# Attention and two feed-forward layers on one core: the order of the five queues comes from an event calculation instead of from hand-set delays

## The chip, the cores and the metric

The kernel runs on one core of a Trainium2 chip. A core has five engines with a queue of instructions each: TensorE (PE, matrix products), ScalarE (ACT), VectorE (DVE), GpSimd (POOL) and SyncE (SP), which here issues all transfers. Each queue is worked off strictly in the order in which it was written, and an instruction whose input or buffer isn't ready holds up all that stands behind it. The metric is the device time of one execution in microseconds (us), the median of several runs. Lower is better.

## The reference: what is computed

```
scores = q @ k.T / sqrt(64)            # q, k, v: 4 batches x 12 heads x 448 x 64
scores = cap * tanh(scores / cap)
attn   = exp(scores - max);  attn = attn / (sum(attn) + 1e-9)
x  = (attn @ v), heads side by side    # 1792 tokens x 768
h  = relu(x @ w_in);         y = (h * h) @ w_out              # 768 -> 2048 -> 768
gate = sigmoid(y @ w_gate);  val = y @ w_val                  # 768 -> 1536
out  = (gate * val) @ moe2_w_out                              # 1536 -> 768
```

The weights come as 64-bit numbers and are turned into 32-bit numbers on the chip.

## The kernel before, in words

The 48 heads are worked in 24 pairs. For a pair there are four steps of scores (on PE, 112 to 128 keys at a time, then tanh and exp on ACT) and four steps of PV (probabilities times values, on PE). The values carry a column of ones, so PV also gives the sums by which a pair's result must be divided: the result is stored to DRAM (`xd`), the row of sums is loaded again (`sg`), DVE takes the reciprocals (`rr`), they are stored (`rd`), and result and reciprocals are loaded side by side, the reciprocals spread over 64 partitions, and multiplied (`normalize`).

The first 12 pairs (the lead) run alone. The tokens of the layers are worked in two passes. Pass 0 takes the first 768 tokens, in blocks of 256 and 512, and the other 12 pairs' 48 attention steps are strewn between its units; pass 1 takes the last 1024 tokens in two blocks of 512. A unit is one product on PE of 128 output features by a block: 6 (`prod_a`) or 4 (`unit_b`) tiles of 128x128 weights, three matmuls for each tile, since every operand is held as a rounded high part and the rest (`wh` and `wl`, the two halves of `xa` and `gx`). In pass 0 there are 82 weight tiles (keys). For each one `wdma` loads the 64-bit words, `wconv` makes 32-bit numbers of them (ACT takes the absolute value, L310, DVE does four operations, L311 to L316), `wkeep` stores the result for pass 1, and `wround` splits it (ACT rounds `wh`, L331, POOL subtracts `wl`, L332). Two buffers `raw` hold a weight from `wconv` until both `wkeep` and POOL are done with it, four buffers hold `wh` and `wl`. From pair 13 on the probabilities `pt` (`th` in a pair's last step) are split on DVE as well before PV may use them (`split_scores`, L186 and L187). PV has one accumulator of two banks, which is copied out after a pair's last step (L210 or L212), so the next pair's first PV waits for that copy.

All five queues are written by hand-set rules: `go(us, fn)` moves a clock on by an assumed PE time, `at(delay, fn)` puts a piece of work into a list that is run when the clock has passed its delay, and `weights(u, n)`, called before each unit, writes as many steps of the weights' chain as counters and two fixed delays allow. Nobody asks there whether a buffer is free or an engine busy. The attention steps are put in when the units so far have used up `ATT` = 0.84 of pass 0's assumed time, step by step (`due`).

Of the kernel before, what the change touches and what calls it, by code (L numbers as in the profile page):

```python
# [14 lines left out]
ALU = mybir.AluOpType  # L15

# [12 lines left out]
PT = 11  # L29
WB = 4  # L30
LEAD = 4
ATT = 0.84
# [7 lines left out]
HIGH = float(np.uint32(0x47EFFFFF).view(np.float32))  # L40


@with_exitstack
def attn_mlp_kernel(ctx: ExitStack, tc: tile.TileContext, qk, v, cap, w1, w2, wg, wv, wo, out):
# [10 lines left out]
    def open_pool(name, side):  # L55
        guard = tc.tile_pool(name=name, bufs=1, side=side)
        open_pools[name] = guard, guard.__enter__()
# [26 lines left out]

    st = {}
    more = tc.tile_pool(name="more", bufs=1, space=bass.MemoryType.PSUM, side="right")
    pools = {"more": more.__enter__()}
# [4 lines left out]
    def unit_bank():  # L92
        return pools["units"].tile([P, 512], F32, tag="pn", name="pn", bufs=4)
# [6 lines left out]

    def new_v1(i, dt):
        vt = T("att", "v1", [P, KC, 4, D], dt, NV)
        w = f32(vt) if dt != F32 else vt
        nc.gpsimd.memset(w[:, :, 1:3, :], 1.0)
        return vt

    def new_v2():
        vt = T("att", "v2", [P, KC, 3, D], F32R, NV)
        nc.gpsimd.memset(f32(vt[:, :, 1, :]), 0.0)
        return vt  # L110

    v32, v1, v2 = [], [], []
# [5 lines left out]
    rd = [[dr.tile([2, S], F32, name=f"rd_{b}_{p}") for p in range(NP)] for b in range(B)]  # L118
    RP, RN = 16, 2 * S // 16


    def early(b):
        return b < B // 2

    def pair_tile(n=2):
        return T("att", "pt", [P, 2, S], bufs=PT) if n == 2 else T("att", "th", [P, 1, S], bufs=3)

    def split_tile(n=2):
        return T("att", "pt", [P, 2, S], F32R, bufs=PT) if n == 2 else T("att", "th", [P, 1, S], F32R, bufs=3)


    def load_pair(b, p):
        qr = T("mlp0", "acc", [P, QK], bufs=CC) if early(b) else T("att", "qk", [P, QK], bufs=2)
        nc.sync.dma_start(out=qr, in_=qk[b, p])
        vr = None
        if not early(b):
            vr = T("att", "vr", [P, KC, 2, D])
            nc.sync.dma_start(out=vr, in_=v[b, p])
        st["raw", b, p] = qr, vr

    def load_v(b, p):
        i = (b * NP + p) % NV
        for j in range(2):
            nc.sync.dma_start(out=v32[i][:, :, 3 * j, :], in_=v[b, p][:, :, j, :])

    def split_pair(b, p):
        qr, vr = st.pop(("raw", b, p))
        hi = T("att", "qkh", [P, QK], F32R, 2)
        lo = T("att", "qkl", [P, QK], F32R, 2)
        if early(b):  # L150
            nc.vector.tensor_copy(hi, qr)
        else:
            nc.scalar.activation(out=hi, in_=qr, func=AF.Copy)
        nc.vector.tensor_tensor(out=lo, in0=qr, in1=f32(hi), op=ALU.subtract)
        st["qk", b, p] = hi, lo
        st["vr", b, p] = vr

    def split_v(b, p):
        i = (b * NP + p) % NV
        vr = st.pop(("vr", b, p))  # L160
        if vr is not None:
            va, vb = v1[i][:, :, 0::3, :], v2[i][:, :, 0::2, :]
            nc.scalar.activation(out=va, in_=vr, func=AF.Copy)
            nc.vector.tensor_tensor(out=vb, in0=vr, in1=f32(va), op=ALU.subtract)


    def scores(b, p, step):
        hi, lo = st["qk", b, p]
        n = 2 if step < 3 else 1
        rows = [slice(0, D), slice(D, P)] if step < 3 else [slice(0, P)]  # L170
        turn = (p + b * NP + step) % 3
        sc = bank2("so" if turn == 0 else "si", pools["more"]) if early(b) and turn < 2 else bank2("se")
        c0 = S + step * P
        for i, (w, a) in enumerate(((lo, hi), (hi, lo), (hi, hi))):
            for u, r in enumerate(rows):
                nc.tensor.matmul(out=sc[:, u, :S], lhsT=w[r, c0:c0 + P], rhs=a[r, :S], start=i == 0, stop=i == 2)
        t = pair_tile(n)
        nc.scalar.activation(out=t, in_=sc[:, :n, :S], func=AF.Tanh, scale=qs)
        nc.scalar.activation(out=t, in_=t, func=AF.Exp, scale=capa)
        st["p", b, p, step] = t, None  # L180

    def split_scores(b, p, step):
        t, _ = st["p", b, p, step]
        n = 2 if step < 3 else 1
        ph, pl = split_tile(n), split_tile(n)
        nc.vector.tensor_copy(ph, t)  # L186
        nc.vector.tensor_tensor(out=pl, in0=t, in1=f32(ph), op=ALU.subtract)  # L187
        st["p", b, p, step] = ph, pl

    def pv(b, p, step):  # L190
        i = (b * NP + p) % NV
        if step == 0:
            st["o", b, p] = bank2("pv")
        o = st["o", b, p]
        ph, pl = st.pop(("p", b, p, step))
        c = (step + 1) % KC
        terms = [(v32, ph)] if early(b) else [(v2, ph), (v1, pl), (v1, ph)]
        for n, (vt, pt) in enumerate(terms):
            for j in range(2):

                r, u = (slice(0, P), j) if step < 3 else (slice(j * D, (j + 1) * D), 0)
                x = j if vt is v2 else 2 * j
                w = vt[i][r, c, x:x + 2, :].rearrange("p x d -> p (x d)")
                nc.tensor.matmul(  # L204
                    out=o[:, j, :S], lhsT=w, rhs=pt[r, u], start=step == 0 and n == 0, stop=step == 3 and n == len(terms) - 1)
        if step < 3:
            return
        xe = st["xe", b, p] = pair_tile()
        if early(b):
            nc.vector.tensor_copy(xe, o[:, :, :S])  # L210
        else:
            nc.scalar.activation(out=xe, in_=o[:, :, :S], func=AF.Copy)  # L212

    def store_pair(b, p):
        xe = st.pop(("xe", b, p))
        for j in range(2):
            r0, e0 = (XR, D - 1) if j else (1, 0)
            nc.sync.dma_start(out=xd[b][p][r0:r0 + D + 1], in_=xe[e0:e0 + D + 1, j])

    def load_sums(b, p):  # L220
        sg = st["sg", b, p] = T("att", "sg", [RP, RN], bufs=2)
        nc.sync.dma_start(out=sg, in_=xd[b][p][XR - 1:XR + 1].rearrange("r (i s) -> (r i) s", s=RN))

    def recips(b, p):
        sg = st.pop(("sg", b, p))
        rr = st["rr", b, p] = T("att", "rr", [RP, RN], bufs=2)
        nc.vector.tensor_scalar(out=sg, in0=sg, scalar1=eps[:RP], scalar2=None, op0=ALU.add)
        nc.vector.reciprocal(rr, sg)

    def store_recips(b, p):  # L230
        nc.sync.dma_start(out=rd[b][p].rearrange("r (i s) -> (r i) s", s=RN), in_=st.pop(("rr", b, p)))

    def hilo_act(dst, src):
        nc.scalar.activation(out=dst[:, 0], in_=src, func=AF.Copy)  # L234

    def hilo_sub(dst, src):
        nc.vector.tensor_tensor(out=dst[:, 1], in0=src, in1=f32(dst[:, 0]), op=ALU.subtract)  # L237

    xn = [dr.tile([P, 2, WIDTH[1]], F32, name=f"xn_{p}") for p in range(NP)]


    def load_pair_result(b, p, c0, c1):
        n = c1 - c0
        if early(b):
            xt = T("mlp0", "acc", [P, QK], bufs=CC)
            xt = xt[:, :2 * S].rearrange("p (x s) -> p x s", x=2)
        else:
            xt = pair_tile()
        st["xt", b, p, c0] = xt
        for j in range(2):  # L250
            rows = slice(j * D, (j + 1) * D)
            cols = slice(c0 - b * S, c1 - b * S)
            nc.sync.dma_start(out=xt[rows, 0, :n], in_=xd[b][p][j * XR + 1:j * XR + 1 + D, cols])
            nc.sync.dma_start(out=xt[rows, 1, :n], in_=rd[b][p][j, cols].unsqueeze(0).to_broadcast((D, n)))


    def normalize(b, p, c0, c1):
        n, t0 = c1 - c0, PASSES[1][0]
        xt = st.pop(("xt", b, p, c0))
        xu, bc = xt[:, 0, :n], xt[:, 1, :n]  # L260
        if c1 <= t0:
            if ("x", 0, p) not in st:
                st["x", 0, p] = T("mlp0", "xa", [P, 2, WIDTH[0]], F32R, CC)
            dst = st["x", 0, p][:, :, c0:c1]
        else:
            dst = st["xs", b, p, c0] = split_tile()[:, :, :n]
        nc.vector.tensor_tensor(out=xu, in0=xu, in1=bc, op=ALU.mult)
        if early(b):
            nc.vector.tensor_copy(dst[:, 0], xu)
        else:  # L270
            hilo_act(dst, xu)
        hilo_sub(dst, xu)

    def store_normalized(b, p, c0, c1):
        t0 = PASSES[1][0]
        nc.sync.dma_start(out=xn[p][:, :, c0 - t0:c1 - t0], in_=f32(st.pop(("xs", b, p, c0))))

    def xload(p, c):
# [402 lines left out]
```

## Time and profile before

| | |
|---|---|
| median of 3 runs | 1487.82 us (1487.71 to 1493.65) |
| the profiled execution's own time | 1488.93 us |
| its span, first to last instruction | 1487.1 us |
| mean granted TensorE clock | 0.916 of full speed |
| busy: PE, DVE, ACT, POOL | 1265.4, 620.4, 597.6, 265.3 us |
| transfers | 160.93 MB, 108 GB/s over the span |

PE is the busiest engine with 85% of the span, but its matmuls are longer where the granted clock is low, so busy time is not work. Idle time of another engine matters only where PE waits for it in the end.

### The profile page before, as it was taken

What the parts mean: (1) busy time and instruction counts of PE and PEld (TensorE: products, weight loads), DVE (VectorE), ACT (ScalarE), POOL (GpSimd) and SP (SyncE); (2) the same over time, 40 slices, a digit from 0 to 9 for tenths busy, and PEclk for the clock granted to TensorE, in tenths of its full rate; (3) what the DMA queues carried; (4) which work ended last, traced back from release to release, by engine and by line L of the source; (5) the groups of instructions that cost most, each with busy time, mean ns of one, the idle gap of its engine ahead of it and who ended that gap; (6) DMA issues with size and microseconds to landing.
All of it is one profiled execution on the core that took longest, in us unless ns stands there. A gap on an engine that the chain in (4) does not pass through costs nothing. (4 is left out here: it accounts for less than half of the span.)

```text
span 1487.1 us, 15573 instructions
## 1 busy us (share of the span) xinstructions
PE 1265.4 (85%) x5880; PEld 1013.9 (68%) x5880; DVE 620.4 (42%) x917; ACT 597.6 (40%) x872; POOL 265.3 (18%) x174
## 2 busy tenths in 40 slices
PE   7756686787688676976797797999999999999998
PEld 4423465576577555765586686888888888888887
DVE  3454454466566454635566763102121521022122
ACT  7663344453634435543563431533324322221210
POOL 0010012012121111112111221231222221222211
PEclk9987788799888887987899898999999999999999
DMA  4554334344445343334443556211111111211112
GB/s 127 160 176 132 94 106 140 117 138 154 146 120 168 95 149 128 113 118 155 134 133 130 173 179 225 91 58 50 43 55 44 58 51 29 75 33 45 62 36 92
DMA packets 79995, 160.93 MB, mean 108 GB/s; under 512 B 22272, under 2 KB 38448, under 8 KB 79920
## 3 DMA queue, kind: packets, MB, share of 16 engines
q1 hardware_dynamic: 79920, 159.94, 33.8%
q8 instruction: 46, 0.75, 0.2%
q14 instruction: 29, 0.24, 0.0%
HBM read 115.69 MB, written 44.21 MB: 108 GB/s over the span
## 5 line engine op out<-in xcount | busy, mean ns | idle before, releaser
L332 POOL TENSOR_TENSOR wl<-raw,wh 128x512 fp32r<-128x512 f32 (+1 forms) x164 | 262.5, 1601 | 1145.9 <-ACT wh L331 983.4
L337 PE MATMUL pn<-xa,wl 128*128 128x512 f32 (+1 forms) x960 | 354.7, 369 | 1.5 <-ACT xa L234 1.5
L338 PE MATMUL pn<-xa,wh 128*128 128x512 f32 (+1 forms) x960 | 352.9, 368 | 2.8 <-DVE xa L237 2.8
L339 PE MATMUL pn<-xa,wh 128*128 128x512 f32 (+1 forms) x960 | 351.7, 366 | 0.0
L204 PE MATMUL pv<-pt,v 128*128 128x448 f32 x360 | 150.9, 555 | 146.4 <-DVE pt L186 100.5
L337 PE MATMUL pn<-gx,wl 128*128 128x512 f32 (+1 forms) x672 | 256.1, 381 | 15.3 <-ACT gx L234 9.8
L338 PE MATMUL pn<-gx,wh 128*128 128x512 f32 (+1 forms) x672 | 255.3, 380 | 15.7 <-DVE gx L237 15.5
L339 PE MATMUL pn<-gx,wh 128*128 128x512 f32 (+1 forms) x672 | 252.5, 376 | 0.0
L331 ACT ACTIVATE wh<-raw 128x512 fp32r<-128x512 f32 (+1 forms) x164 | 119.4, 729 | 273.6 <-PE pn L339 147.5
L204 PEld LDWEIGHTS pv<-pt,v 128*128 128x128 f32 x360 | 78.7, 238 | 201.3 <-issue 71.2
L337 PEld LDWEIGHTS pn<-xa,wl 128*128 128x128 f32 x960 | 185.4, 193 | 34.4 <-issue 3.5
L338 PEld LDWEIGHTS pn<-xa,wh 128*128 128x128 f32 x960 | 185.3, 193 | 31.9 <-DVE xa L237 3.4
L339 PEld LDWEIGHTS pn<-xa,wh 128*128 128x128 f32 x960 | 184.7, 192 | 28.9
L337 PEld LDWEIGHTS pn<-gx,wl 128*128 128x128 f32 x672 | 136.1, 203 | 40.2 <-ACT gx L234 10.6
L338 PEld LDWEIGHTS pn<-gx,wh 128*128 128x128 f32 x672 | 135.5, 202 | 38.9 <-DVE gx L237 18.2
L310 ACT ACTIVATE raw<-w 128x512 f32<-128x512 f32 (+1 forms) x82 | 64.0, 781 | 231.4 <-POOL wl L332 99.2
L237 DVE TENSOR_TENSOR gx<-g,gx 128x512 fp32r<-128x512 f32 (+1 forms) x112 | 85.1, 772 | 169.5 <-ACT gx L234 169.2
L339 PEld LDWEIGHTS pn<-gx,wh 128*128 128x128 f32 x672 | 135.1, 201 | 21.4
L311 DVE TENSOR_SCALAR raw<-raw 128x512 f32<-128x512 f32 (+1 forms) x82 | 41.8, 509 | 258.4 <-ACT raw L310 258.4
L392 DVE TENSOR_TENSOR acc<-pn,acc 128x512 f32<-128x512 f32 (+1 forms) x120 | 74.0, 620 | 142.8 <-PE pn L339 142.6
L374 DVE TENSOR_TENSOR g<-pn,r 128x512 f32<-128x512 f32 (+1 forms) x48 | 29.3, 617 | 173.1 <-PE pn L339 173.1
L314 DVE SCALAR_TENSOR_TENSOR raw<-w,raw 128x512 uint32<-128x512 uint32 (+1 forms) x82 | 79.0, 964 | 2.8
(72 smaller groups left out, 998.4 us busy)
## 6 DMA issues: line engine op xcount, KB each, us to landing
w<-in_w_dram SPq DMA_DIRECT2D x16, 768.0 KB
w<-in_w_dram SPq DMA_DIRECT2D x24, 512.0 KB
w<-in_wg_dram SPq DMA_DIRECT2D x12, 768.0 KB
w<-in_wv_dram SPq DMA_DIRECT2D x12, 768.0 KB
w<-in_wo_dram SPq DMA_DIRECT2D x18, 512.0 KB
s_w<-raw SPq DMA_DIRECT2D x16, 384.0 KB
s_w<-raw SPq DMA_DIRECT2D x24, 256.0 KB
xa<-xn SPq DMA_DIRECT2D x12, 512.0 KB
```

Source lines behind the costliest of these rows:

```text
L204: nc.tensor.matmul(out=o[:, j, :S], lhsT=w, rhs=pt[r, u], start=step == 0 and n == 0, stop=step == 3 and n == len(terms) - 1)
L237: nc.vector.tensor_tensor(out=dst[:, 1], in0=src, in1=f32(dst[:, 0]), op=ALU.subtract)
L310: nc.scalar.activation(out=raw, in_=hi.bitcast(F32), func=AF.Abs)
L311: nc.vector.tensor_scalar(out=raw, in0=raw, scalar1=LOW, scalar2=HIGH, op0=ALU.max, op1=ALU.min)
L314: nc.vector.scalar_tensor_tensor(out=mu, in0=lo, scalar=29, in1=mu, op0=ALU.logical_shift_right, op1=ALU.bitwise_or)
L331: nc.scalar.activation(out=hi_, in_=raw, func=AF.Copy)
L332: nc.gpsimd.tensor_tensor(out=lo_, in0=raw, in1=f32(hi_), op=ALU.subtract)
L337: nc.tensor.matmul(out=o, lhsT=wl, rhs=hi, start=first, stop=False)
L338: nc.tensor.matmul(out=o, lhsT=wh, rhs=lo, start=False, stop=False)
L339: nc.tensor.matmul(out=o, lhsT=wh, rhs=hi, start=False, stop=last)
L374: nc.vector.tensor_tensor(out=g, in0=pa, in1=st.pop(("r", off)), op=ALU.mult)
L392: nc.vector.tensor_tensor(out=acc, in0=pb, in1=acc, op=ALU.add)
```

## The change

The work on ACT, DVE and POOL is the same but for small things. What is new is a class `Flow` in the kernel's source: a small calculation of events, run while the program is written. It has a clock, counts of free buffers, and for each of ACT, DVE, POOL and SP a queue in which pieces of work with a rank wait until the engine is free; durations are formulas (`act`, `dve`, `landing`). Each chain of work is a job that says `take` (wait for a free buffer), `until` (wait for an event), `for` (wait for a time) or `on` (run on an engine). An instruction is written to its queue at the moment at which the calculation starts it. PE is served by `pick`: the lead's list first, with pass 0's units allowed between; then an attention step if it is due by `ATT` = 0.86, or if no unit can run and the step can; else the next unit. A unit is written when its weights, inputs and one of four banks are there by the calculation.

The small things: a pair's result and reciprocals are loaded with two transfers instead of four (eight for the pairs that token 768 cuts); the absolute value and the rounding of the first four weights are done on DVE instead of ACT; a weight's store follows its conversion at once instead of at the next conversion; pass 0's first four weights' units run block by block; the second pass's inputs are loaded with 2 us between them.

```diff
-        waits = (1.2, 2.5, 2.5, 0.5, 2.5, 2.5, 2.0) if fast else (1.5, 4.0, 4.0, 1.0, 4.0, 5.0, 3.0)
-        d = 0.0
-        for wait, fn in zip(waits, (store_pair, load_sums, recips, store_recips)):
-            d += wait
-            at(d, fn, b, p)
-    def weights(u, n):
-        while len(at_round) < len(at_conv) and len(at_round) < n + 4:
-            m = len(at_round)
-            if now[0] < at_conv[m] + 2.5 or m >= WB and last[keys[m - WB]] >= u:
-                break
-            key = keys[m][1:]
-            wround(key)
...
+class Flow:
+    def serve(self, engine):
+        if not self.free[engine] or not self.queue[engine]:
+            return
+        _, _, _, length, write, job = heapq.heappop(self.queue[engine])
+        self.free[engine] = False
+        write()
+        length = length() if callable(length) else length
...
+        self.at(self.now + length, end)
...
+    def act(n):
+        return 0.23 + n * 0.00083
+    def dve(self, n):
+        return lambda: (0.15 + n * 0.00104) * (1.0 if self.free["POOL"] else 1.6)
...
+    def landing(self, size, store=False, rate=330e3):
+        begin = max(self.now + (0.5 if store else 0.95), self.pipe)
+        self.pipe = begin + size / rate
+        return self.pipe + 0.6 - self.now
...
+        yield act(t, t, AF.Exp, 0, 0.06, scale=capa)
+        if early(n):
+            st["p", n, step] = t, None
+        else:
+            yield "take", kind
+            ph = score_tile(step, F32R)
+            yield copy(ph, t, 0)
...
+        def load():
+            nc.sync.dma_start(out=xt[:, 0], in_=y)
+            nc.sync.dma_start(out=xt[:, 1], in_=rd[b][p].unsqueeze(1).to_broadcast((2, D, S)))
...
+        flow.put("w64")
...
+        flow.spawn(keep(key, raw))
+        yield from round_w(m, raw, 0.0, ("kept", key))
...
+        yield "until", ("w", m - 1) if m else ("t", WSTART, 3)
+        yield "take", "wh"
...
+        yield copy(hi, raw) if m < WB else act(hi, raw)
+        yield on("POOL", 0.15 + n * 0.0023, lambda: nc.gpsimd.tensor_tensor(out=lo, in0=raw, in1=f32(hi), op=ALU.subtract))
...
+            unit_ok = done(("w", u["m"]), *u["needs"]) and have("pn")
+        if step_ok and (pe["done"] >= i * gap or not unit_ok):
```

The first place is DVE's queue at the 17th of the 48 attention steps. `pt` are probabilities (the CAST makes the high part, the subtraction below it the rest), `raw<-w` are conversions of a weight, `gx` and `acc` belong to units. Before:

```order
L237 TENSOR_TENSOR gx<-g,gx 128x256
L311 TENSOR_SCALAR raw<-raw 128x512
L312 TENSOR_SCALAR raw<-raw 128x512
L314 SCALAR_TENSOR_TENSOR raw<-w_2798,raw 128x512
L316 SCALAR_TENSOR_TENSOR raw<-w_2798,raw 128x512
L186 CAST pt<-pt 128x896
L187 TENSOR_TENSOR pt<-pt 128x896
```

Now:

```order
L503 TENSOR_SCALAR raw<-raw 128x512
L215 TENSOR_TENSOR gx<-g,gx 128x256
L505 SCALAR_TENSOR_TENSOR raw<-w_2712,raw 128x512
L507 SCALAR_TENSOR_TENSOR raw<-w_2712,raw 128x512
L606 TENSOR_TENSOR acc<-pn,acc 128x256 x2
L218 CAST pt<-pt 128x896
L215 TENSOR_TENSOR gx<-g,gx 128x512
L215 TENSOR_TENSOR pt<-pt 128x896
```

The same kinds of work stand there, but the conversion is now cut into by the units' work, and the next weight's first operation stands behind the split.

The second place is ACT's queue just ahead of that step. `wh` is the rounding of a weight (POOL's subtraction follows it and frees a `raw`), `raw<-w` the first operation on a later weight (it needs the freed `raw`), `r`, `g`, `gx` are a unit's results. Before:

```order
L359 ACTIVATE r<-pn 128x512
L360 ACTIVATE g<-r 128x512
L234 ACTIVATE gx<-g 128x512
L331 ACTIVATE wh<-raw 128x512
L310 ACTIVATE raw<-w_3312 128x512
L359 ACTIVATE r<-pn 128x256
```

Now:

```order
L212 ACTIVATE r<-pn 128x256
L212 ACTIVATE raw<-w_2712 128x512
L212 ACTIVATE g<-r 128x256
L212 ACTIVATE gx<-g 128x256
L212 ACTIVATE wh<-raw 128x512
L212 ACTIVATE r<-pn 128x512
L212 ACTIVATE g<-r 128x512
L212 ACTIVATE pt<-se,qs 128x896
L212 ACTIVATE pt<-pv 128x896
L212 ACTIVATE pt<-pt,capa 128x896
L212 ACTIVATE gx<-g 128x512
L212 ACTIVATE raw<-w_2775 128x512
```

Before, `raw<-w` stood right behind `wh`; now six instructions stand between them.

The third place is SP's queue in the lead, where a pair's result and reciprocals come back. `xd` and `rd` are as above, `v` and `qk` the inputs of coming pairs, `s_w` the stores of weights. Before:

```order
L253 DMA acc<-xd_0_91 64x320
L254 DMA acc<-rd_0_115 64x320
L253 DMA acc<-xd_0_91 64x320
L254 DMA acc<-rd_0_115 64x320
L253 DMA acc<-xd_0_91 64x128
L254 DMA acc<-rd_0_115 64x128
L253 DMA acc<-xd_0_91 64x128
L254 DMA acc<-rd_0_115 64x128
L218 DMA xd_1_92<-pt 65x448 x2
```

Now:

```order
L480 DMA w_985<-in_w_dram 128x1024
L222 DMA s_w_0_0_987<-raw 128x512
L222 DMA sg<-xd_2_93 16x56
L410 DMA acc<-xd_0_91 128x1x448
L411 DMA acc<-rd_0_115 128x1x448
L410 DMA acc<-xd_1_92 128x1x448
L411 DMA acc<-rd_1_116 128x1x448
L222 DMA sg<-xd_3_94 16x56
```

Eight transfers of one pair have become two, and two pairs come back together.

## Rows read from the trace of the kernel before

**Rows 1.** Busy us (instructions) by stretch: PE, PEld, DVE, ACT, POOL; clock, DMA share, GB/s.
```profile
0.00:167.00 167.00, 114.62 (x444) 65.01 (x444) 74.52 (x125) 95.59 (x110) 9.35 (x11) 0.87 0.47 142
167.00:926.30 759.30, 594.80 (x2991) 489.83 (x2990) 422.42 (x639) 340.62 (x502) 131.86 (x83) 0.87 0.43 139
926.30:1487.10 560.80, 555.94 (x2449) 459.08 (x2447) 123.47 (x153) 161.44 (x260) 124.04 (x80) 1.00 0.18 57
```

**Rows 2.** Timeline of PE: start, us, instruction, idle time before it and its releaser.
```profile
6.61 0.74 PE L176 MATMUL so<-qkh,qkl 64*128 64x448 f32 x2 [6.61 <-DVE qkl L154]
...
21.37 0.72 PE L176 MATMUL se<-qkh,qkl 64*128 64x448 f32 x2
...
29.51 0.72 PE L176 MATMUL so<-qkh,qkl 64*128 64x448 f32 x2
...
408.03 2.89 PE L204 MATMUL pv<-pt,v 128*128 128x448 f32 x6 [8.43 <-DVE pt L186]
...
418.70 0.28 PE L337 MATMUL pn<-gx,wl 128*128 128x256 f32 x1
...
420.02 0.28 PE L339 MATMUL pn<-gx,wh 128*128 128x256 f32 x1
420.23 0.47 PE L176 MATMUL se<-qkh,qkl 64*128 64x448 f32 x2
...
422.35 0.28 PE L337 MATMUL pn<-gx,wl 128*128 128x256 f32 x1
```

**Rows 3.** What PE waited for, 0 to 926.3 us: total us, times, longest.
```profile
PE pv L204 <- DVE pt L186: 100.5, 22, 9.2
PE pv L204 <- DVE pt L210: 34.1, 8, 9.9
PE pv L204 <- DVE th L186: 18.9, 5, 11.6
PE pn L338 <- DVE gx L237: 14.2, 4, 7.3
PE pn L337 <- ACT gx L234: 9.8, 4, 6.5
...
PE pv L204 <- DVE pt L187: 4.8, 11, 0.5
```

**Rows 4.** Timeline of ACT ahead of the PE wait that ends at 408.03.
```profile
398.72 1.04 ACT L179 ACTIVATE pt<-pt,capa 128x896 f32<-128x896 f32 x1
...
404.32 0.66 ACT L310 ACTIVATE raw<-w 128x512 f32<-128x512 f32 x1 [1.42 <-POOL wl L332]
```

**Rows 5.** Timeline of DVE there and 13 us later.
```profile
405.01 0.43 DVE L311 TENSOR_SCALAR raw<-raw 128x512 f32<-128x512 f32 x1 [6.76 <-ACT raw L310]
...
407.27 0.62 DVE L186 CAST pt<-pt 128x896 fp32r<-128x896 f32 x1
407.92 1.09 DVE L187 TENSOR_TENSOR pt<-pt 128x896 fp32r<-128x896 f32 x1
...
420.40 1.92 DVE L314 SCALAR_TENSOR_TENSOR raw<-w,raw 128x768 uint32<-128x768 uint32 x1
422.35 0.96 DVE L316 SCALAR_TENSOR_TENSOR raw<-w,raw 128x768 uint32<-128x768 uint32 x1
```

**Rows 6.** POOL beside the last two.
```profile
419.84 1.66 POOL L332 TENSOR_TENSOR wl<-raw,wh 128x512 fp32r<-128x512 f32 x1 [1.60 <-ACT wh L331]
```

**Rows 7.** What DVE waited for, 0 to 926.3 us: total us, times, longest.
```profile
DVE raw L311 <- ACT raw L310: 258.4, 68, 9.5
DVE acc L267 <- DMA acc<-rd: 45.0, 14, 6.3
...
DVE sg L227 <- DMA sg<-xd: 20.9, 8, 4.8
```

**Rows 8.** The chain that ended last, 845 to 900 us: first and last of four conversions.
```profile
862.78 0.68 ACT raw L310
...
897.05 0.67 ACT raw L310
```

More of the change, by code (lines that the diff above doesn't have):

```diff
@@ L132, in load_pair @@
[L132 to L144, printed above, removed]
@@ L156, in split_pair @@
[L156 to L169, printed above, removed]
+        yield copy(hi, qr, 0) if early(n) else act(hi, qr)
@@ L190, in pv, with softmax @@
-    def pv(b, p, step):
-        i = (b * NP + p) % NV
+            for x, r in enumerate(rows):
+                nc.tensor.matmul(out=sc[:, x, :S], lhsT=w[r, c0:c0 + P], rhs=a[r, :S], start=i == 0, stop=i == 2)
+        if early(n) and n == lead - 1 and step == 3:
+            close_pool("more")
+            open_pool("units", "right", space=bass.MemoryType.PSUM)
+            flow.at(flow.now, lambda: flow.fire("units"))
+        return softmax(n, step, sc[:, :u, :S])
+    def softmax(n, step, sc):
+        if step == 3:
+            flow.put("qkh")
+        kind = "pt" if step < 3 else "th"
+        yield "take", kind
+        t = score_tile(step)
+        yield act(t, sc, AF.Tanh, 0, 0.02, scale=qs)
+        flow.put("sb")
+        flow.fire(("free", n, step))
+        yield act(t, t, AF.Exp, 0, 0.06, scale=capa)
+        if early(n):
+            st["p", n, step] = t, None
+        else:
+            yield "take", kind
+            ph = score_tile(step, F32R)
+            yield copy(ph, t, 0)
+            yield "take", kind
+            pl = score_tile(step, F32R)
+            yield sub(pl, t, f32(ph), 0)
+            flow.put(kind)
+            st["p", n, step] = ph, pl
+        flow.fire(("t", n, step))
@@ L262, in normalize @@
+        for x0, x1 in ((c0, min(c1, T0)), (max(c0, T0), c1)):
+            if x0 < x1:
+                yield from normalize(n, x0, x1, xt[:, 0, x0 - c0:x1 - c0])
+        flow.put(kind)
+    def normalize(n, c0, c1, xu):
+        p = pairs[n][1]
+        w = c1 - c0
+        if c1 <= T0:
             if ("x", 0, p) not in st:
+                yield "take", "xa0"
                 st["x", 0, p] = T("mlp0", "xa", [P, 2, WIDTH[0]], F32R, CC)
@@ L265, in normalize @@
         else:
[L266 to L269, printed above, removed]
[L270 to L281 removed]
+            yield "take", "pt"
@@ new lines, in products @@
+    def products(m, n, operand, off, w):
+        wh, wl = st["w", m]
+        o = open_pools["units"][1].tile([P, 512], F32, tag="pn", name="pn", bufs=4)[:, :w]
+        for i in range(n):
+            s = slice(i * P, (i + 1) * P)
+            a = operand(i)
+            hi, lo = a[:, 0, off:off + w], a[:, 1, off:off + w]
+            nc.tensor.matmul(out=o, lhsT=wl[:, s], rhs=hi, start=i == 0, stop=False)
+            nc.tensor.matmul(out=o, lhsT=wh[:, s], rhs=lo, start=False, stop=False)
+            nc.tensor.matmul(out=o, lhsT=wh[:, s], rhs=hi, start=False, stop=i == n - 1)
+        return o
@@ new lines, in val, with unit_b @@
+    def val(k, off, w, f, o):
+        yield "until", ("r", k, f, off)
+        yield "take", f"g{k}"
+        g = T(f"mlp{k}", "g", [P, SP], bufs=2)[:, :w]
+        yield on("DVE", flow.dvep(w), lambda: nc.vector.tensor_tensor(out=g, in0=o, in1=st["r", k, f, off], op=ALU.mult))
+        flow.put("pn")
+        flow.put(f"r{k}")
+        yield from split_g(k, off, w, F1 + f, g)
+    def unit_b(u, kind, k, off, w, gi, c, ng):
+        o = products(u["m"], FG, lambda i: st["g", k, gi * FG + i + (F1 if kind == "wo" else 0)], off, w)
+        return total(kind, k, off, w, gi, c, ng, o)
@@ L428, in drain @@
-    def drain():
-        while waiting:
-            now[0] = max(now[0], waiting[0][0])
-            run()
-    NS = 1.0 / 1000
+        yield on("DVE", flow.dvep(w), lambda: nc.vector.tensor_tensor(out=acc, in0=o, in1=acc, op=ALU.add))
+        flow.put("pn")
+        if gi < ng - 1:
+            return
+        if kind == "w2":
+            if ("y", k, c) not in st:
+                yield "take", f"xa{k}"
+                st["y", k, c] = T("mlp0" if k == 0 else "act1", "xa", [P, 2, WIDTH[k]], F32R, CC)
+            dst = st["y", k, c][:, :, off:off + w]
+            yield act(dst[:, 0], acc)
+            yield sub(dst[:, 1], acc, f32(dst[:, 0]))
+            flow.fire(("y", k, c, off))
+        else:
+            t0 = PASSES[k][0] + off
+            yield from dma(out[:, c, t0:t0 + w], acc, P * w * 4, True, issue=0.33)
@@ L528, in attn_mlp_kernel @@
-    pairs = [(b, p) for b in range(B) for p in range(NP)]
-    lead = NP * B // 2
-    engines = {mybir.EngineType.PE, mybir.EngineType.Activation, mybir.EngineType.DVE, mybir.EngineType.Pool, mybir.EngineType.SP}
-    manual = tc.manual_schedule(engines=engines)
-    manual.__enter__()
-    v32 += [new_v1(i, F32) for i in range(NV)]
-    load_pair(*pairs[0])
-    load_v(*pairs[0])
-    load_pair(*pairs[1])
-    split_pair(*pairs[0])
+    last = {u["m"]: i for i, u in enumerate(units)}
+    ends = {}
@@ new lines, in attn_mlp_kernel @@
+    for i, u in enumerate(units):
+        k, kind, x = u["key"]
+        if kind == "w1":
+            ends["xa", k, "x"] = i
+        elif kind == "wv":
+            ends["xa", k, "y"] = i
+        elif kind in ("w2", "wo"):
+            ends["gx", k, kind, x[0]] = i
+    freed = {}
+    for (kind, k, *_), i in ends.items():
+        freed.setdefault(i, []).extend([f"{kind}{k}"] * (FG if kind == "gx" else CC))
+    pass0 = sum(u["us"] for u in units if u["key"][0] == 0)
+    n0 = sum(u["key"][0] == 0 for u in units)
@@ L564, in attn_mlp_kernel @@
-    pools["units"] = more.__enter__()
-    v1 += [new_v1(i, F32R) for i in range(NV)]
-    v2 += [new_v2() for i in range(NV)]
-    its = []
-    for b, p in pairs[lead:]:
-        for s in range(4):
-            its.append((b, p, s))
-    total = sum(u[0] for u in units if u[1][0] == 0)
-    gap = ATT * total / len(its)
-    due = [(0.3, 0.8)[i] * gap if i < 2 else i * gap for i in range(len(its) + 1)]
-    done = 0.0
-    i = 0
-    xs = [(p, c) for c in (0, SP) for p in range(NP)]
-    k0 = 0
@@ L612, in attn_mlp_kernel, with have, done, run_pe @@
-    drain()
-    manual.__exit__(None, None, None)
+            order += [("V", n - 1, 1), ("V", n - 1, 2), ("V", n - 1, 3)]
+    steps = [(n, s) for n in range(lead, len(pairs)) for s in range(4)]
+    pe = {"busy": False, "a": 0, "u": 0, "i": 0, "done": 0.0}
+    gap = ATT * pass0 / len(steps)
+    def have(*res):
+        return all(flow.have[r] > 0 and not flow.taking.get(r) for r in res)
+    def done(*events):
+        return all(x in flow.done for x in events)
+    def run_pe(length, lag, after):
+        pe["busy"] = True
+        def end():
+            pe["busy"] = False
+            flow.at(flow.now + lag, after)
+            pick()
+        flow.at(flow.now + length, end)
@@ new lines, in turn_over, with pass_end, banks @@
+    def turn_over():
+        yield "for", 3.0
+        close_pool("mlp0")
+        open_pool("mlp1", "left")
+        flow.fire("mlp1")
+    def pass_end(job):
+        yield "until", "mlp1"
+        yield from job
+    def banks():
+        for s in (1, 2):
+            yield "until", ("free", lead - 1, s), "units"
+            flow.put("pn")
+            flow.put("pn")
+    flow.changed = pick
+    with tc.manual_schedule(engines={ENGINES.PE, ENGINES.Activation, ENGINES.DVE, ENGINES.Pool, ENGINES.SP}):
+        for job in (load_qk(), load_v(), load_w(), load_x(), banks()):
+            flow.spawn(job)
+        flow.run()
@@ L614, in attn_mlp_kernel @@
+    assert pe["u"] == len(units) and pe["i"] == len(steps) + 1
     close_pool("mlp1")
     close_pool("act1")
-    more.__exit__(None, None, None)
+    close_pool("units")
 _OUTS = [((P, CC, B * S), "float32")]
```

704 lines of the change are left out of this document (397 added, 307 removed).

## The prediction

> **What bounds the kernel now.** I read the busy time by stretch first. The span falls into the lead with its last PV (0 to 167 us), pass 0 with the other pairs' attention (to 926.3) and pass 1 (560.8 us) [rows 1]. In pass 1 PE is busy for 555.94 of 560.8 us at clock 1.00: PE is the bound there. The order of PE's rows in pass 1 is the same in both programs, so I keep 560.8 us as it stands. In the first two stretches PE is busy for 114.62 + 594.80 = 709.4 of 926.3 us, so it is idle for 216.9 us, and its clock is 0.87.
>
> Next, how much of the 709.4 us is work at full clock. A pair of the lead takes 8.14 us (29.51 - 21.37) [rows 2]: 12 pairs are 97.7 us. Pass 0 has 96 + 96 + 144 + 72 = 408 weight tiles by block, so 1224 matmuls of 256 columns and 1224 of 512. Eleven of the former lie in 420.02 - 418.70 = 1.32 us, 0.12 us each [rows 2], and one of the latter takes 555.94 / 2449 = 0.227 us [rows 1]: 146.9 + 277.8 = 424.7 us. An attention step takes 422.35 - 420.23 = 2.12 us [rows 2]; of a pair's four steps one has half the scores and one half the PV, so 12 x 3.5 x 2.12 = 89.0 us. Together 611 us. The other 709.4 - 611 = 98 us of busy time are matmuls at the lower clock, which come after idle time: 98 / 216.9 = 0.45 us for each idle us. So the time to pass 1 is 611 + 1.45 x I, with I the idle time of PE (611 + 1.45 x 216.9 = 925.5, as measured). All that this change can give lies in I.
>
> Then the waits of PE [rows 3]: 100.5 + 18.9 us are 27 waits of PV for the DVE cast of the probabilities, 34.1 us are 8 waits of the lead's PV for the copy of the accumulator on DVE, and 24.0 us are units waiting for inputs of their own pass. What the first kind is made of is seen at 408.03, where PE waited for 8.43 us. The exp had been done at 399.76 (398.72 + 1.04) [rows 4], yet the cast ran at 407.27, since a weight's conversion stood ahead of it on DVE, which waited for 6.76 us [rows 5] for ACT's L310 at 404.32, and that for POOL [rows 4]. So no engine was short of time; one queue's head waited for another's. DVE waited for that L310 258.4 us in 68 waits [rows 7].
>
> **The change part by part.** The work hardly changes, and PE's order hardly either: by the printed order the last PV stands behind 370 us of pass 0's units (at the durations above), before behind 360. So whatever is gained comes from the orders of ACT, DVE, POOL and SP. I cost I anew.
>
> *The start*, 6.61 us until the first split operand [rows 2], stays: 6.6.
>
> *PV waiting for the cast* (119.4 us): the cast is now written when the calculation has the exp done and DVE free, and a conversion's first DVE operation only when it has L310 done. As long as these times hold to about a us, no conversion waits at DVE's head for long. What stays is what PE waits where the cast is in time: 4.8 us in 11 waits on the subtraction, 0.44 us each [rows 3]. For all 48 steps 21 us.
>
> *PV waiting for the accumulator's copy* (34.1 us, all while weights are converted in the lead): adding DVE's durations along the new order, 49 us stand between the sixth and the twelfth copy, against 6 x 8.14 = 48.8 us on PE. DVE is just full there, also because four absolute values and four roundings come over from ACT. A copy can find an operation of 0.96 us [rows 5] ahead of it: 6 x 0.96 = 6 us. Without this cover (DVE over full by a us a pair) it would be 12.
>
> *Units waiting for gx*, 14.2 + 9.8 us [rows 3]: the chain from a product through ACT and DVE is as it was: 24 us stay.
>
> *Pass 0's opening*: by the new PE order four attention steps stand there with no unit between. From its scores to its PV a step needs 0.8 + twice 1.04 (tanh taken as long as exp) + 0.62 + 1.09 = 4.6 us [rows 4, 5], with the PV 5.9; two overlap, in which PE works 4.2: 0.85 us idle a step, with the one before it 4 us, taken as 5.
>
> *Fewer transfers for the sums*: 72 transfers fewer on SP ahead of pass 1's inputs. SP is not on the path, so this itself is 0; the cover is SP's idle time. But DVE stands at the head of its queue for the sums and the products of each pair: 45.0 + 20.9 = 65.9 us in 22 waits until now [rows 7]. Now it stands there 48 times at moments that a formula gives. The bounds: nothing, or 48 x 65.9 / 22 = 144 us if each waits as those 22 and all of it reaches PE. DVE has free time between (496.9 us of 926.3 busy [rows 1]), and a wait that ends before the next cast is due costs nothing, so I take the lower end's side: 0.25 us each, 12 us.
>
> *The weights*: six instructions now stand between ACT's rounding and the next L310, so ACT no longer waits for POOL with everything behind it; the stores follow at once. Cost 0, covered as long as a key comes faster than PE uses one.
>
> Sum: I = 6.6 + 21 + 6 + 24 + 5 + 12 = 74.6. Time to pass 1: 611 + 1.45 x 74.6 = 719 us; span 719 + 560.8 = 1280. The profiled execution took 1488.9 with a span of 1487.1, the median of the runs is 1487.8, so 0.7 over the span: **1280 us**.
>
> **The rivals.**
>
> *PE hardly idle*: only start and gx stay, I = 31, 611 + 45 + 561 = 1217 us. For it: nothing in the engines' sums forbids it, DVE has 497 us of work for 611. Against it: each of the 48 PV waits for a chain over two engines.
>
> *DVE becomes the bound*: DVE's L314 took 1.92 us beside POOL's subtraction, which ran until 421.50, and the next like it 0.96 [rows 5, 6]; so an operation that meets POOL starts only behind it. The denser the two lie, the more of POOL's 9.35 + 131.86 = 141 us is added to DVE's 497: at most 638, over PE's 611. With the idle time of the forecast (108 us) on top, 746 + 561 = 1307. The Trainium skill (SBUF — State Buffer, Who interferes with whom) says that a VectorE instruction with both inputs in SBUF contends with a GpSimd instruction that reads SBUF, and that one of the two blocks fully instead of both being slowed; the row agrees (1.92 against 0.96), while the calculation in the source has a factor of 1.6. By that rule the time to pass 1 could not be under 638 us where all of it meets, and the rival before this one would fall out.
>
> *Transfers hold up DVE*: half of the 144 us reach PE, I = 62.6 + 72 = 135: 611 + 195 + 561 = 1367; all of it, 1473. For it: the longest of these waits were 6.3 and 4.8 us [rows 7], and nothing in the formula knows how full the transfer queues are. Against it: until now most of them stood in the lead.
>
> *Slower, by the weights' chain*: a key must pass two `raw` buffers. At the end of pass 0 the chain that ended last went through these alone: three periods in 897.05 - 862.78 = 34.3 us, 11.4 us a key [rows 8]. Where all 82 keys come like that, from 60 us on, pass 1 begins at 60 + 82 x 11.4 = 995 and the time is 1556. It decides from (926.3 - 60) / 82 = 10.6 us a key. Against it: in these 11.4 us a store waits for the next conversion to be written, and that is undone.
>
> *Nothing changes*: PE's order is the old one, and the waits at the heads of queues come back elsewhere in the old sum: 1488.
>
> **How the numbers follow.** Chances: forecast (1240 to 1330) 0.52, DVE as bound 0.10, PE hardly idle 0.15, transfers 0.15, slower 0.05, no change 0.03. The range 1215 to 1370 takes in the first three and half of the fourth; it leaves out 0.08 + 0.05 + 0.03 and a little below 1215. Within 0.5% (7 us, about what the runs can tell from no change) 0.03, slower 0.05, faster 0.92.
>
> **What would show it.** In the profile after: PE's waits for the cast of `pt` at about 20 us instead of 119, those for the accumulator's copy under 10; the clock over the time to pass 1 near 0.95; pass 1 at 561 us; the wait of DVE's first conversion operation for ACT down from 258 us to under a third. I am wrong if DVE's waits for `rd`, `xd` or `sg` grow over 100 us, if DVE is busy for nearly the whole of pass 0, or if pass 1 gets longer, on which I have put nothing.

## The result, and the profile after

The changed kernel takes 1339.52 us (median of 4 runs, 1338.37 to 1339.88), the kernel before 1489.3 us beside it; the ratio is 0.8989 (95% interval 0.8967 to 0.901). The profiled execution has a span of 1338.0 us at a mean granted clock of 0.954. That is 60 us above the forecast of 1280 and inside the range, but not for the reasons of the forecast.

The busy time by stretch of the changed kernel, with the columns of [rows 1]; pass 1 begins at 778 us:

```profile
0.00:778.00 778.00, 665.77 (x3429) 524.79 (x3430) 524.01 (x766) 422.62 (x605) 152.47 (x93) 0.92 0.54 167
778.00:1338.00 560.00, 555.91 (x2453) 459.99 (x2451) 121.67 (x153) 164.93 (x261) 126.31 (x81) 1.00 0.18 55
```

Pass 1 is as before (560.0 us). The whole gain lies ahead of it: 926.3 - 778 = 148 us. There PE is idle for 778 - 665.8 = 112.2 us (216.9 before), where the forecast had 74.6. The eight largest of what PE waited for in these 778 us (total us, times, longest):

```profile
PE pv L369 <- DVE pt L218: 38.5, 11, 10.2
PE pv L369 <- DVE xa L215: 11.9, 1, 11.9
PE pv L369 <- DVE pt L215: 11.9, 11, 2.4
PE pv L369 <- DVE pt L382: 11.4, 4, 4.8
PE pv L369 <- DVE th L218: 6.8, 3, 6.4
PE so L325 <- DVE qkl L215: 6.6, 1, 6.6
PE pn L544 <- DVE gx L215: 4.8, 5, 2.7
PE pn L543 <- ACT gx L212: 4.7, 3, 2.3
```

Many lines share a helper, so the tile tells what it is: `pt` or `th` at L218 is the cast of the probabilities, at L215 the subtraction behind it, `pt` at L382 the copy of the accumulator. The waits for the cast fell from 119 us [rows 3] to 38.5 + 6.8 = 45, not to 20. The first three lines of the same view for DVE:

```profile
DVE acc L415 <- DMA acc<-rd: 69.3, 11, 8.8
DVE pt L415 <- DMA pt<-rd: 56.9, 11, 7.9
DVE raw L501 <- ACT raw L212: 33.4, 29, 2.9
```

The wait that led the list before, that of the conversion for ACT's first operation, went from 258.4 us [rows 7] to 33.4. At the top there is now another one: DVE stands for 126.2 us, 22 times, at the product of a pair's result with its reciprocals, because the load of `rd` has not landed. Before, such waits came to 47.9 us in 15: the 45.0 us of [rows 7] and one of 2.9 us at the `pt` of a later pair.

The single wait of 11.9 us that the view of PE puts down to `xa` is of this kind too: it ends at 129.40 us, behind a product that had waited for `rd` until 126.71 us. How such waits reach PE is seen best in the opening of pass 0. DVE's timeline, then PE's:

```profile
173.81 0.63 DVE L415 TENSOR_TENSOR acc<-acc 128x448 f32<-128x448 f32 x1 [8.83 <-DMA acc<-rd]
...
175.25 0.62 DVE L218 CAST pt<-pt 128x896 fp32r<-128x896 f32 x1
```

```profile
160.56 2.90 PE L369 MATMUL pv<-pt,v 128*128 128x448 f32 x6 [6.93 <-DVE pt L218]
...
175.92 3.00 PE L369 MATMUL pv<-pt,v 128*128 128x448 f32 x6 [10.17 <-DVE pt L218]
```

DVE waits for 8.83 us with the product at its head, the cast stands behind it, and PE waits 10.17 us for that cast. PE pays twice, by its clock:

```profile
150.00:200.00 50.00, 19.67 (x73) 12.73 (x72) 18.25 (x42) 10.97 (x17) 0.00 (x0) 0.57 0.31 102
```

In these 50 us PE works for 19.67 us only, and the granted clock averages 0.57, near the lower of its two levels (1.2 of 2.4 GHz). The transfers that DVE waits for are seen in the chain that ended last (start, us, what):

```profile
103.80 0.55 SPq L410
104.39 0.79 SPq L411
105.23 4.45 SPq L410
109.72 16.90 DMA acc<-rd
126.71 0.62 DVE acc L415
...
138.77 17.65 DMA acc<-rd
156.45 0.63 DVE acc L415
```

Two pairs come back together, four loads of 224 KB. The last lands 17 us after SP came to its issue, which itself lasts some 4.4 us instead of 0.6. Where the loads of one pair are in flight with only a store beside them, from 194 to 204 us, the view of the transfers (tenths of 16 transfer engines, then GB/s, in 40 slices of 0.25 us) reads as below; the two rows of SP's timeline behind it are the issues of that pair's loads.

```profile
DMA  1111111211111119711111111111111111111110
GB/s 43 49 50 57 43 57 43 90 50 50 50 50 50 50 65 318 234 43 57 43 57 43 57 50 50 50 50 50 50 57 43 57 43 57 50 50 50 45 35 14
DMA packets 566, 0.61 MB, mean 61 GB/s; under 512 B 25, under 2 KB 565, under 8 KB 565
...
acc<-rd SPq DMA_DIRECT2D x1, 224.0 KB
xn<-pt SPq DMA_DIRECT2D x1, 128.0 KB
```

```profile
187.49 0.49 SPq L410 DMA_DIRECT2D acc<-xd  x1
...
194.61 0.49 SPq L411 DMA_DIRECT2D acc<-rd  x1
```

The hump of 318 GB/s is the store of `xn`, 0.13 MB. The other 0.48 MB of the 0.61, at about 50 GB/s and a tenth of the engines, are two loads of 0.23 MB: the result's, issued at 187.49 us behind earlier ones, and the reciprocals'. The chain puts down 9.25 us (from 194.61) to the latter, but two loads were worked off in that time. From these bytes one of them takes an estimated 4.6 us, and two at once get no more than 50 GB/s together. So the loads are slow by themselves, and they also queue behind each other: four are an estimated 18 us, and the last of four above landed after 17. That is a part of the change that the forecast priced at 12 us: "a pair's result and reciprocals are loaded with two transfers instead of four".

Theory A: the joined loads are slow for their shape, and without them the new order would leave PE hardly idle. Rivals: the form of the loads is harmless, and the new order issues them in one burst and puts the products to DVE's head too early (theory B); the loads are slow since they are larger or fewer; the gain comes from something other than the calculation's times. A second question is how slow loads cost PE time: by DVE standing at its head for them (theory H), or by what comes late behind them whatever DVE does (theory L).

### The profile page after: what moved, and what is told of

The parts are those of the page before. It is cut to its first block, busy times and chain, and to the rows that moved or that the text cites. A ratio compares the mean times of both kernels' runs of the same rounds, so it can differ in the third digit from the quotient of the medians.

```text
span 1338.0 us, 15427 instructions
## 1 busy us (share of the span) xinstructions
PE 1221.7 (91%) x5880; PEld 984.8 (74%) x5880; DVE 645.7 (48%) x919; ACT 587.6 (44%) x866; POOL 278.8 (21%) x174
## 4 chain that ended last, share of the span: by engine, by line
PE 51%; DMA 25%; DVE 13%; ACT 4%; issue 3%; SPq 2%; POOL 0%; ACTq 0%; DVEq 0%; POOLq 0%
PE pn L544 16%; PE pn L543 16%; PE pn L545 16%; DMA acc<-rd 6%; DMA pt<-rd 5%; DMA s_w<-raw 4%; DMA rd<-rr 3%; DMA s_wv<-raw 3%; DVE raw L505 2%; PE pv L369 2%; DVE raw L507 2%; DVE raw L501 2%; DMA s_wo<-raw 2%; DVE pt L215 1%; DMA xd<-pt 1%
## 5 line engine op out<-in xcount | busy, mean ns | idle before, releaser
L528 POOL TENSOR_TENSOR wl<-raw,wh 128x512 fp32r<-128x512 f32 (+1 forms) x164 | 276.0, 1684 | 1001.2 <-ACT wh L212 762.8
L544 PE MATMUL pn<-gx,wh 128*128 128x512 f32 (+1 forms) x672 | 246.9, 367 | 4.9 <-DVE gx L215 4.8
L543 PE MATMUL pn<-gx,wl 128*128 128x512 f32 (+1 forms) x672 | 246.8, 367 | 4.8 <-ACT gx L212 4.7
L545 PE MATMUL pn<-gx,wh 128*128 128x512 f32 (+1 forms) x672 | 245.4, 365 | 0.0
L369 PE MATMUL pv<-pt,v 128*128 128x448 f32 x360 | 132.8, 503 | 77.3 <-DVE pt L218 38.5
L369 PEld LDWEIGHTS pv<-pt,v 128*128 128x128 f32 x360 | 70.9, 212 | 122.5 <-DVE pt L218 36.6
L215 DVE TENSOR_TENSOR gx<-g,gx 128x512 fp32r<-128x512 f32 (+1 forms) x112 | 83.8, 749 | 160.0 <-ACT gx L212 160.0
L543 PEld LDWEIGHTS pn<-gx,wl 128*128 128x128 f32 x672 | 128.4, 191 | 27.7 <-ACT gx L212 6.4
L544 PEld LDWEIGHTS pn<-gx,wh 128*128 128x128 f32 x672 | 128.3, 191 | 26.7 <-DVE gx L215 7.0
L545 PEld LDWEIGHTS pn<-gx,wh 128*128 128x128 f32 x672 | 128.3, 191 | 20.0
L212 ACT ACTIVATE gx<-g 128x512 fp32r<-128x512 f32 (+1 forms) x112 | 64.4, 575 | 68.9 <-DVE g L588 67.1
L212 ACT ACTIVATE r<-pn 128x512 f32<-128x512 f32 (+1 forms) x112 | 59.9, 535 | 69.6 <-PE pn L545 64.5
```

What stands on the lines that cost most here:

```text
L212: return on("ACT", flow.act(cols(out)) + extra, lambda: nc.scalar.activation(out=out, in_=in_, func=func, **kw), rank)
L215: return on("DVE", flow.dve(cols(out)), lambda: nc.vector.tensor_tensor(out=out, in0=a, in1=b, op=ALU.subtract), rank)
L369: nc.tensor.matmul(out=o[:, j, :S], lhsT=w, rhs=pt[r, u], start=step == 0 and m == 0, stop=step == 3 and m == len(terms) - 1)
L528: yield on("POOL", 0.15 + n * 0.0023, lambda: nc.gpsimd.tensor_tensor(out=lo, in0=raw, in1=f32(hi), op=ALU.subtract))
L543: nc.tensor.matmul(out=o, lhsT=wl[:, s], rhs=hi, start=i == 0, stop=False)
L544: nc.tensor.matmul(out=o, lhsT=wh[:, s], rhs=lo, start=False, stop=False)
```

## The experiments

**e1_four: the changed kernel with four loads for a pair.** For each half j of the 128 rows the load is issued apart, as before the change; all else is the change.

```diff
-            nc.sync.dma_start(out=xt[:, 0], in_=y)
-            nc.sync.dma_start(out=xt[:, 1], in_=rd[b][p].unsqueeze(1).to_broadcast((2, D, S)))
+            for j in range(2):
+                rows = slice(j * D, (j + 1) * D)
+                nc.sync.dma_start(out=xt[rows, 0], in_=xd[b][p][j * XR + 1:j * XR + 1 + D])
+                nc.sync.dma_start(out=xt[rows, 1], in_=rd[b][p][j].unsqueeze(0).to_broadcast((D, S)))
```

> The kernel after, with a pair's result and reciprocals loaded by four transfers (one per head of the pair) as before, and the order of everything else as in the kernel after. Theory A (the combined loads are slow by their form: DVE stands 126 us at its head for them, and in pass 0's opening 41 us of that reach PE): DVE's waits for these loads fall under 40 us, PE's idle time by some 35 to 50 us, the time to 1265 to 1290 us. Theory B (the loads are late because two pairs' loads, weights and stores are issued in one burst and the formula puts the product too early; the form is harmless): the waits stay over 90 us and the time is 1330 to 1350 us, since SP issues 48 transfers more.

Measured: 1219.26 us, ratio to the kernel before 0.8178 (0.8156 to 0.82). It beats both kernels, and it fell further than theory A said (1265 to 1290); theory B (1330 to 1350) falls. Its stretches, and all of PE's waits of half a us or more ahead of pass 1, which begins at 658:

```profile
0.00:658.20 658.20, 630.31 (x3431) 508.03 (x3432) 525.51 (x766) 422.91 (x606) 158.38 (x93) 0.99 0.65 198
658.20:1217.10 558.90, 555.28 (x2450) 459.46 (x2448) 121.74 (x153) 164.72 (x261) 126.24 (x81) 1.00 0.18 55
```

```profile
PE pv L369 <- DVE pt L218: 7.4, 6, 1.9
PE so L325 <- DVE qs L185: 6.8, 1, 6.8
PE pv L369 <- DVE pt L215: 6.6, 8, 2.4
PE pv L369 <- DVE th L218: 3.1, 1, 3.1
PE pv L369 <- DVE pt L382: 1.9, 3, 1.1
PE pv L369 <- DMA v<-in_v_dram: 1.0, 1, 1.0
PE pv L369 <- DVE th L215: 0.5, 2, 0.3
```

PE is idle for 27.9 us and the clock is 0.99. DVE now waits for `rd` for 7.6 + 6.6 us in 9 waits. The spans differ by 1338.0 - 1217.1 = 120.9 us, PE's idle time by 112.2 - 27.9 = 84.3: 1.43 us of time for each idle us.

**e2_rd_two and e3_xd_two: one kind of load at a time.** In the first only the load of the reciprocals is cut by rows again, in the second only that of the result.

```diff
             nc.sync.dma_start(out=xt[:, 0], in_=y)
-            nc.sync.dma_start(out=xt[:, 1], in_=rd[b][p].unsqueeze(1).to_broadcast((2, D, S)))
+            for j in range(2):
+                nc.sync.dma_start(out=xt[j * D:(j + 1) * D, 1], in_=rd[b][p][j].unsqueeze(0).to_broadcast((D, S)))
```

> Only the reciprocals' load is split by head, the result's load stays one transfer. If under theory A the spread load (two DRAM rows, each to 64 partitions) is the slow one: 1265 to 1290 us as with four transfers. If the result's load is slow, or both: over 1310 us. Theory B: 1330 to 1345 us.

> Only the result's load is split by head, the reciprocals' load stays one spread transfer. If the spread load is the slow one: 1330 to 1345 us, DVE's waits as in the kernel after (about 126 us). If the result's load is slow: 1265 to 1290 us.

Measured: 1251.85 us with the result joined, 1273.58 with the reciprocals joined (one run each). The first lies below everything that was expected of it, as e1_four does; the second lies where the result's load was to be the slow one. Over e1_four they cost 33 and 54 us, so both kinds are slow, and both together (120) cost more than the sum of 87. That they hold up each other fits the view above, where two in flight share 50 GB/s. DVE waits for the loads at the product for 29.8 + 17.5 us in the one and 32.0 + 25.6 us in the other.

**e4_before_one: the kernel before, with only its loads joined.**

```diff
-        for j in range(2):
-            rows = slice(j * D, (j + 1) * D)
...
+        nc.sync.dma_start(out=xt[:, 0, :n], in_=y)
+        nc.sync.dma_start(out=xt[:, 1, :n], in_=rd[b][p][:, cols].unsqueeze(1).to_broadcast((2, D, n)))
```

> The kernel before with the combined loads of the kernel after (two transfers instead of four or eight) and its own hand-set order. Theory A: each load is 7 us or more later than before, the hand-set delays of 4 to 5 us don't cover it, DVE's waits for it grow from 48 us to over 120 us and the time to 1510 to 1570 us. Theory B: the form is harmless, 1475 to 1495 us.

Measured: 1633.73 us (one run), 143 us slower than the kernel before. DVE's waits there (L266 is the product):

```profile
DVE acc L266 <- DMA acc<-rd: 109.5, 15, 13.4
DVE pt L266 <- DMA pt<-rd: 33.3, 5, 11.3
```

So the loss belongs to the loads, not to the new order: in the old one they cost even more (143 us against 120), and more than was expected (1510 to 1570 us).

**e5_true_landing: the loads stay joined, but the calculation knows of it.** By theory H the loads cost time because DVE stands at their head with the casts behind it. Then most of it should come back if the product is written when the load really lands.

```diff
-        yield "for", flow.landing(2 * P * S * 4, rate=170e3)
+        yield "for", 8.0 + flow.landing(2 * P * S * 4, rate=170e3)
```

> The kernel after with its slow combined loads, but the event calculation is told 8 us more for them, which is about what the trace shows, so the product is written later in DVE's queue. Theory H (the loads cost because DVE stands at their head with the casts behind): DVE's waits for them fall from 126 to under 50 us and the time to 1240 to 1290 us. Theory L (what costs is that the normalized inputs come late, and SP's blocked issues): 1310 us or more.

Measured: 1328.99 us (one run), some 10 us less than the change. DVE's waits for `rd` at the product fell from 126.2 to 12.2 us, but others came. Of DVE's rows, and the first two of PE's:

```profile
DVE raw L501 <- ACT raw L212: 73.5, 28, 9.5
DVE sg L397 <- DMA sg<-xd: 44.5, 8, 10.2
...
DVE acc L415 <- DMA acc<-rd: 12.2, 2, 6.2
```

```profile
PE pv L369 <- DVE pt L218: 32.2, 8, 8.3
PE pv L369 <- DMA v<-in_v_dram: 24.7, 5, 11.2
```

The load of the sums, which stands behind these loads on SP, is late instead (44.5 us), and so is that of the values, for which PE now waits 24.7 us. So theory H falls, and the time lies in the range of theory L (1310 us or more): what comes late behind the loads costs about as much as DVE standing there.

**e10_cols: four loads, but cut along the columns.** As many transfers and bytes as e1_four, 112 KB each, but each still spans 2 x 64 rows.

```diff
-            nc.sync.dma_start(out=xt[:, 0], in_=y)
-            nc.sync.dma_start(out=xt[:, 1], in_=rd[b][p].unsqueeze(1).to_broadcast((2, D, S)))
+            for h0, h1 in ((0, S // 2), (S // 2, S)):
+                nc.sync.dma_start(out=xt[:, 0, h0:h1], in_=y[:, :, h0:h1])
+                nc.sync.dma_start(out=xt[:, 1, h0:h1], in_=rd[b][p][:, h0:h1].unsqueeze(1).to_broadcast((2, D, h1 - h0)))
```

> The changed kernel with the loads of the sums as four transfers per pair again, but cut along the columns: each still has an outermost dimension of 2 (2 x 64 rows) and half the columns, 112 KB. If these loads are slow for their shape (few transfer engines work on a transfer whose outermost dimension is 2), the time stays at 1300 to 1360 and DVE's waits for rd stay over 80 us. If they are slow because one transfer is too large or because there are too few of them in flight, it falls to 1215 to 1250 as with the four transfers cut by rows.

Measured: 1353.68 us, ratio 0.9077 (0.9057 to 0.9096); 134 us over e1_four, 14 over the change. DVE waits ahead of pass 1:

```profile
DVE acc L416 <- DMA acc<-rd: 74.3, 11, 9.0
DVE pt L416 <- DMA pt<-rd: 66.6, 12, 8.6
```

It isn't the size and isn't the number. Nor is it the length of a row, which is half as long here, since the change with its whole rows is as slow. It is that a transfer's outermost dimension is 2. The rows of a pair's two halves don't follow each other in DRAM (rows of sums lie between them), and the reciprocals are one row for each half, repeated 64 times; so in this layout one transfer for both was written as 2 x 64 rows. The Trainium skill (DMA: Bandwidth & Descriptors, Rules for kernel authors) says just this: a transfer uses at most as many of the 16 engines as its outermost dimension is long, and a small one confines it. The tenth of the engines and the 50 GB/s in the view above agree. By the 27 GiB/s for an engine in the Trainium skill (DMA: Bandwidth & Descriptors, Specifications), two would give an estimate of 58 GB/s. The trace's rows do not name the engines, so that it is two is taken from the share: from 190 to 194 us of the changed kernel, with only these loads in flight, it is 13.1% (the line's last number), and 2 of 16 is 12.5%.

```profile
q1 hardware_dynamic: 119, 0.20, 13.1%
```

Another layout in DRAM, with which a joined transfer has a longer outermost dimension, wasn't tried.

**e6_half: is it the calculation's times?** e1_four with the durations of ACT and DVE halved in the formulas, so that the calculation still knows the buffers and the dependences, but not how long work lasts.

```diff
-        return 0.23 + n * 0.00083
+        return 0.5 * (0.23 + n * 0.00083)
```

(and likewise in the three formulas of DVE)

> The kernel with four transfers (1219 us) whose event calculation takes all durations on ACT and DVE at half. Theory O (the order is good because its times are right to about a us): queues are written as if work were done early, heads wait again, 1270 us or more. Theory S (what counts is that buffers and inputs are respected at all, the durations matter little): 1215 to 1245 us.

Measured: 1288.11 us (one run), 69 us over e1_four, in the range of theory O. But the conversions still wait little for ACT (32.7 us), and three quarters of the gain are there with times that are half of what they should be. Queues' heads wait more again: DVE waits for `gx` 29.4 us against 6.5 in e1_four, PE for the cast of `pt` 21.7 against 7.4.

**e7_due: no attention step in a gap.** e1_four with PE's rule cut to the due time:

```diff
-        if step_ok and (pe["done"] >= i * gap or not unit_ok):
+        if step_ok and pe["done"] >= i * gap:
```

> The kernel with four transfers (1219 us), but an attention step is put on PE only when it is due, never because no unit can run. If, as the prediction has it, PE's order gives next to nothing: 1215 to 1235 us. If the steps in gaps are a main part of the gain: over 1250 us.

Measured: 1228.67 us, ratio 0.8242 (0.8211 to 0.8272): 0.8% over e1_four. Steps in gaps give about 9 us of the 270.

**e8_store_late: the weights' stores late again.** e1_four, where a weight's store of pass 0 is issued only when the next conversion begins.

```diff
+        flow.fire(("start", m))
...
+    def keep(m, key, raw):
+        if keys[m + 4][0] == 0:
+            yield "until", ("start", m + 1)
```

> The kernel with four transfers (1219 us), but a weight's store is issued only once the next weight's conversion begins, as in the kernel before. If the late store was a large part of the old chain of 11.4 us a key: over 1250 us. If two raw buffers have room for it when the order is right: 1215 to 1235 us.

Measured: 1227.59 us (1219.0 to 1229.71), ratio 0.8236 (0.8217 to 0.8254), and a profiled span of 1217.2, that of e1_four: so some 8 us or less.

**e9_before_keep: the stores at once, in the old order.** The kernel before, with the call that stores a weight moved behind its conversion:

```diff
-                keep(m - 1)
                 wconv(keys[m][1:])
+                keep(m + 1)
```

> The kernel before with its own hand-set rules; only the store of each converted weight is issued right behind its conversion, not ahead of the next one. If the late stores were what held the weights' chain (the reason given against the rival of the weights' chain), DVE's first conversion operation waits less for ACT than 258 us and the time falls to 1440 to 1480. If the waits come from the heads of the queues, as the order of ACT and DVE sets them, the time stays within 1% of the kernel before (1475 to 1500).

Measured: 1502.02 us, ratio 1.0073 (1.005 to 1.0095), so slightly slower than before and within 1% of it, as the second reading had it. The conversion's wait for ACT went from 258.4 us [rows 7] to 213.8, but DVE's for the sums from 20.9 to 53.5. That the early stores hold up the sums' loads on SP is likely, but not shown.

```profile
DVE raw L311 <- ACT raw L310: 213.8, 61, 10.0
DVE sg L227 <- DMA sg<-xd: 53.5, 16, 7.6
```

## Why the prediction was right and wrong

**What bounds the kernel, and the price of idle time: right.** Pass 1 is 560.0 us (561 forecast), and only I moved. From the idle time measured, 611 + 1.45 x 112.2 = 774 us stands against 778 for the change, and 611 + 1.45 x 27.9 = 651 against 658 for e1_four. So nearly all that went wrong lies in the terms of I.

**The term that failed: "Fewer transfers for the sums ... this itself is 0", then "0.25 us each, 12 us".** It counted transfers and priced the waits by the loads of before; the edit's second half, that the joined load has another shape, was not priced at all. DVE waited 126 us in 22 waits, 5.7 us each, where the upper bound took 48 of 3.0. e1_four shows what that cost PE: 84 us of idle time, 121 us of time. The prediction's own sign for being wrong, DVE's waits for `rd` over 100 us, came true. The rival *Transfers hold up DVE* had the place right, but of the cause only a part: the loads do queue, but behind each other, and because each is slow by its shape. The time lies between that rival and the forecast.

**The other terms were too large, and hid half of that.** Without the joined loads I is 27.9 us, not the 62.6 of the remaining terms: 35 x 1.45 = 50 us too much, while the loads were 72 x 1.45 = 105 us too little; 1280 - 50 + 105 = 1335. That the time fell into the range is luck: two errors of opposite sign. By name: the waits for cast and subtraction are 17.6 us in e1_four (forecast 21: right), the opening is in these already (5 was put on top), the copy 1.9 (6). The large one is `gx`: "24 us stay" is wrong, since no unit waits for it in e1_four's list. The chain from a product to `gx` is as it was, but the calculation writes a unit on PE when its inputs should be there. The forecast looked at the chain and not at who chooses. No run took this apart by itself. The prediction also put some 28 us of smaller waits of before at nothing without a reason; in e1_four 1.4 us are left of them.

**The rival *PE hardly idle*, 1217 us, is what the new order gives by itself** (1219), but by its number more than by its sum: it kept 24 us for `gx` and nothing for the cast. What was held against it, that each PV waits for a chain over two engines, costs 17.6 us for 48 steps once that chain is written in time.

***DVE becomes the bound*: no.** DVE is busy for 525.5 us of 658 in e1_four, 28.6 more than before [rows 1], part of which is the work taken over from ACT; the 141 us that the rival could add did not come. How much of DVE's work meets POOL's was not taken apart.

**The weights.** Cost 0 holds: the conversion waits 33.4 us for ACT. The reason given against *the weights' chain*, the store issued at once, does not carry it: alone it gains nothing (e9), and without it 8 us at most are lost (e8). What broke that chain is the new order of ACT and DVE, and it doesn't take exact times: in e6 the conversions still wait for ACT for 32.7 us only.

**What stays open:** how the 203 us between the kernel before and e6_half divide among the calculation's knowledge of buffers, of dependences and of half-right times was not taken apart. Nor were the other small things, such as the first four weights' work on DVE, tried alone.

## What to carry to other kernels

Fewer transfers are not cheaper by count: look at the outermost dimension of the joined one first, and cut by rows rather than join two blocks that do not follow each other. In a kernel of in-order queues, ask of each wait not only how long the chain behind it is but what stands at the head of the queue that it goes through; in e1_four an order that was calculated from buffers, dependences and times, with its small things, took 271 us off. And if a change holds a good and a bad part, the sum hides both: run the parts apart before keeping the whole.

## What was not expected of the hardware

Two loads of 224 KB, each as 2 x 64 rows, were worked off in 9.25 us with only a store beside them, at about 50 GB/s with a tenth of the transfer engines at work, and the last of four landed 17 us after SP came to its issue. In e1_four four loads of 112 KB, which carry a whole pair, were issued from 104.17 us on, and the product ran at 110.55 without a wait:

```profile
104.17 0.59 SPq L412 DMA_DIRECT2D acc<-xd  x1
105.01 0.45 SPq L413 DMA_DIRECT2D acc<-rd  x1
105.60 0.49 SPq L412 DMA_DIRECT2D acc<-xd  x1
106.14 0.59 SPq L413 DMA_DIRECT2D acc<-rd  x1
...
110.55 0.60 DVE L417 TENSOR_TENSOR acc<-acc 128x448 f32<-128x448 f32 x1
```

The slow loads also block the queue that issues them. In the changed kernel, with two in flight, the issue of the third and of the fourth took 4.45 and 4.41 us, about the estimated 4.6 us of one such load, against 0.45 to 0.59 us in e1_four. Everything behind them on SP waited as long.

```profile
109.72 4.41 SPq L411 DMA_DIRECT2D acc<-rd  x1
```
